# A packed feed-forward tail inside the logit group, a two-block K ring, and a re-tuned order: what it does to a kernel that TensorE bounds

## The chip, the cores and the metric

One core of one Trainium2 chip. The metric is the device time of one execution in microseconds (us), the median of several executions. Runs are with a granted TensorE clock of 0.99 or more.

## The reference, cut to what matters

One transformer layer without a second residual step: a layer norm feeds an attention branch and a gated feed-forward branch, and both are added to x. S is 2048, D is 512, 32 heads of 16, each position attends to 8 positions at distance 2, and the feed-forward width is **1376 = 10 x 128 + 96**. The inputs are bfloat16.

```python
x  = A_x
xn = layernorm(x)                       # no scale, no shift
# attention: q, k, v = xn @ wqkv; position s sees s, s-2, ..., s-14 (those >= 0)
logits = einsum("bhsd,bhswd->bhsw", q, k[idx]) * Dh**-0.5
o      = einsum("bhsw,bhswd->bhsd", softmax(masked logits), v[idx])
# feed-forward
h      = gelu(xn @ w_gate) * (xn @ w_up)        # 1376 columns
return x + o @ wo + h @ w_down
```

## The kernel before: the parts that matter

The kernel works on four blocks of 512 positions. A program in Python lists some 770 tasks with their engines, dependences and priorities, schedules them against a model of the chip, and emits each engine's instructions in the order found. So a change of a priority or of a model constant changes the order on every engine. A tile with a number (tile 4) is one of 16 of 128 positions each, four to a block; a column tile is a part of TensorE's array. A join is a place where TensorE needs what another engine has made.

TensorE does these groups: the QKV projection, the gate and up projections (11 pairs per block, the eleventh with 96 columns), the output and down projections (11 steps of 128, the last of 96), and two sorts of sums over products that VectorE has made and keeps in product buffers: the logits (`er`, 32 matmuls) and the value groups (`pvr`, 16 matmuls). The last two use weights of 32 columns, so that four matmuls run side by side on four column tiles. TensorE writes its results to a memory called PSUM, from where ScalarE and VectorE fetch them (an evacuation).

```python
        Wg = sb("Wg", [128, 4, DF], BF)          # DF = 1376
        Wu = sb("Wu", [128, 4, DF], BF)
        KT = sb("KT", [128, 4, PITCH], BF)       # K of all 2048 positions
        UNI = sb("UNI", [128, NUNI, 4, 512], BF) # NUNI = 10 product buffers
# ... the logit group of block b
                def mk_r(grp=list(er_grp), lg=it_lg):
                    def f(e):
                        for (g, prs) in grp:
                            for wq in range(2):
                                for sj in range(4):
                                    ins = e.matmul(PS[32 * sj:32 * sj + 32, ...],
                                        lhsT=E8[:, 24 - 8 * g:56 - 8 * g],
                                        rhs=UNI[:, prs[wq].slot, :, sj * 128:(sj + 1) * 128],
                                        start=(g == 0), stop=(g == 3), tile_position=(0, 32 * sj))
# ... gate and up of block b
            for j in range(NJ):                  # NJ = 11
                M = 128 if j < 10 else DF - 1280 # 96 columns in the last
                # 4 matmuls of 512 columns of x for gate, 4 for up; gelu and a copy on ScalarE,
                # one product on VectorE from SBUF
# ... the start: the order of tiles 0 to 3 on VectorE is fixed by hand
        chain(["bnst0", "bnag0", "ve0", "bnst1", "rstd0", "norm0", "bnag1", "ve1", "sub1", "bnst2", "rstd1",
               "norm1", "bnag2", "ve2", "sub2", "bnst3", "rstd2", "norm2", "bnag3", "ve3", "sub3", "rstd3",
               # ... cut
# ... the end of SyncE's stream
        if eng_name == "sp":
            for (s, tot) in self.dma_totals:     # 24 semaphores
                e.wait_ge(s, tot)
```

## Time and profile before

| | before |
|---|---|
| time, median of 3 runs (range) | 199.36 us (199.34 to 199.66) |
| span in the profile | 197.7 us |
| TensorE / VectorE / ScalarE / GpSimd busy | 97% / 75% / 53% / 6% |
| chain that ended last | 94% TensorE, 3% DMA, 1% VectorE |
| groups of 32-column tiles | 12, which makes 24 changes of tile form |

The first two rows differ by what lies outside the first and last instruction. The row to look at is the chain: from 8.4 us on it stays on TensorE, so the time is the start, plus what TensorE has to stream, plus the stretch after its last matmul. The lines of the profile are in the prediction. Timeline of the kernel before: start, length, engine, line, operation, what ended the idle time before it.

```profile
193.35 1.37 PE L1367 MATMUL PS<-Wd,HT 128*128 128x256 bf16 x11
194.83 0.42 DVE L1387 TENSOR_TENSOR OB<-PS,XR 128x256 bf16<-128x256 f32 x1 [1.19 <-PE PS L1367]
```

The span ends at 197.70, so 2.45 us follow the end of the last addition (195.25).

### The profile page before, as it was taken

The page shows a single profiled execution, that of the slowest core. Times are in us where ns is not written, and L with a number is a line of the kernel's source. Part 1 is how long each engine was busy: PE and PEld are TensorE (multiplying, and loading weights), DVE is VectorE, ACT ScalarE, POOL GpSimd, SP SyncE. Part 2 cuts the span into 40 slices and gives each one's busy share as a digit, 9 for nine tenths or more (in the row PEclk, how much of TensorE's full clock was granted, in tenths as well). Part 3 has the DMA queues.
Part 4 walks back from the last instruction along what each step waited for, and adds up shares of the span by engine and source line. Part 5 has one row for each costly group of instructions (what it writes and reads, how often), then busy time and mean ns, then how long its engine had stood idle before and what let it go on. Part 6 is the DMA issues. An engine that isn't in the chain of part 4 may idle for free.

```text
span 197.7 us, 3146 instructions
## 1 busy us (share of the span) xinstructions
PE 191.9 (97%) x1192; PEld 91.3 (46%) x1192; DVE 149.1 (75%) x230; ACT 105.0 (53%) x171; POOL 11.4 (6%) x32
## 2 busy tenths in 40 slices
PE   7799999999999999999999999999999999999993
PEld 2595444444444444444444444444444444444483
DVE  3789989999989999999879379995692986122131
ACT  4377459976737770075788104776792007776000
POOL 6420010130001000001000000000000000000000
DMA  4999998899327913529992535023953350010121
GB/s 120 363 385 385 276 154 182 224 210 165 108 53 177 224 33 102 159 82 171 222 176 46 119 122 133 0 58 103 234 100 93 89 153 27 0 55 3 53 66 40
DMA packets 33054, 27.02 MB, mean 137 GB/s; under 512 B 9392, under 2 KB 31504, under 8 KB 33040
## 3 DMA queue, kind: packets, MB, share of 16 engines
q1 hardware_dynamic: 33040, 26.83, 56.0%
q8 instruction: 9, 0.15, 0.3%
q14 instruction: 5, 0.04, 0.1%
HBM read 19.99 MB, written 5.26 MB: 128 GB/s over the span
## 4 chain that ended last, share of the span: by engine, by line
PE 94%; DMA 3%; DVE 1%; SPq 1%; issue 0%; DVEq 0%
PE PS L1316 39%; PE PS L1367 19%; PE PS L1087 18%; PE PS L1362 7%; PE PS L1285 4%; PE PS L1158 4%; PE PS L1043 3%; DMA XIN<-in_A_x_dram 3%; PE PS L995 0%; SPq L908 0%; DVE st L923 0%; SPq L860 0%; DVE OB L1387 0%; DVE XIN L970 0%; DVE rstd L946 0%
## 5 line engine op out<-in xcount | busy, mean ns | idle before, releaser
L1316 PE MATMUL PS<-xnT,Wu 128*128 128x512 bf16 (+1 forms) x176 | 44.6, 379 | 0.0
L1316 PE MATMUL PS<-xnT,Wg 128*128 128x512 bf16 (+1 forms) x176 | 44.4, 379 | 0.0
L1367 PE MATMUL PS<-Wd,HT 128*128 128x512 bf16 (+3 forms) x198 | 41.2, 356 | 0.0
L1264 DVE TENSOR_TENSOR UNI<-BS,PT 128x2048 bf16<-128x2048 bf16 x32 | 37.5, 1219 | 2.9 <-DMA PT<-pt_scratch 1.7
L1135 DVE TENSOR_TENSOR UNI<-QT,KT 128x2048 bf16<-128x2048 bf16 x32 | 37.2, 1219 | 0.5 <-PE PS L1285 0.2
L1087 PE MATMUL PS<-xnT,Wqkv 128*128 128x512 bf16 x160 | 36.2, 379 | 0.0
L1333 ACT ACTIVATE UU<-PS 128x512 bf16<-128x512 f32 (+1 forms) x44 | 26.4, 599 | 12.3 <-PE PS L1316 12.3
L1326 ACT ACTIVATE GG<-PS 128x512 bf16<-128x512 f32 (+1 forms) x44 | 26.3, 600 | 10.6 <-PE PS L1316 10.3
L1338 DVE TENSOR_TENSOR HT<-GG,UU 128x512 bf16<-128x512 bf16 (+1 forms) x44 | 17.4, 418 | 16.4 <-ACT UU L1333 16.4
L1367 PEld LDWEIGHTS PS<-Wd,HT 128*128 128x128 bf16 (+1 forms) x198 | 19.4, 98 | 18.7
L1316 PEld LDWEIGHTS PS<-xnT,Wg 128*128 128x128 bf16 (+1 forms) x176 | 17.2, 100 | 21.4 <-issue 1.3
L1316 PEld LDWEIGHTS PS<-xnT,Wu 128*128 128x128 bf16 (+1 forms) x176 | 17.4, 100 | 21.0 <-issue 0.8
L1087 PEld LDWEIGHTS PS<-xnT,Wqkv 128*128 128x128 bf16 x160 | 15.3, 98 | 19.4 <-ACT KT L1104 0.8
L1387 DVE TENSOR_TENSOR OB<-PS,XR 128x512 bf16<-128x512 f32 (+1 forms) x18 | 11.3, 630 | 15.9 <-PE PS L1367 15.9
L1111 ACT ACTIVATE VT<-PS 128x512 bf16<-128x512 f32 x16 | 9.5, 597 | 15.2 <-PE PS L1087 15.2
L1296 ACT ACTIVATE OT<-PS 128x512 bf16<-128x512 f32 x16 | 8.7, 594 | 16.3 <-PE PS L1285 16.3
L1362 PE MATMUL PS<-Wo,OT 128*128 128x512 bf16 (+1 forms) x72 | 16.8, 355 | 0.0
L1097 ACT ACTIVATE QT<-PS 128x512 bf16<-128x512 f32 x12 | 7.2, 597 | 12.7 <-PE PS L1087 12.7
L923 DVE BATCH_NORM_STATS2 st<-XIN 128x6 f32<-128x512 bf16 x16 | 10.4, 684 | 4.2 <-DMA XIN<-in_A_x_dram 4.2
L940 POOL TENSOR_TENSOR sq<-ve,mhalf 128x2 bf16<-128x2 f32 (+1 forms) x10 | 7.6, 763 | 77.7 <-DVE ve L934 77.7
L1362 PEld LDWEIGHTS PS<-Wo,OT 128*128 128x128 bf16 x72 | 7.0, 97 | 7.1
L1214 DVE TENSOR_REDUCE ms<-DE 128x128 f32<-128x1024 f32 x4 | 7.6, 1908 | 2.6 <-ACT DE L1209 2.6
(53 smaller groups left out, 114.9 us busy)
## 6 DMA issues: line engine op xcount, KB each, us to landing
BS<-vt_scratch SPq DMA_DIRECT2D x64, 128.5 KB, 3.3
vt_scratch<-VT SPq DMA_DIRECT2D x16, 128.0 KB
XR<-in_A_x_dram SPq DMA_DIRECT2D x16, 128.0 KB, 2.3
XIN<-in_A_x_dram SPq DMA_DIRECT2D x7, 256.0 KB, 3.9
out_dram<-OB SPq DMA_DIRECT2D x14, 128.0 KB, 2.0
Wqkv<-in_A_wqkv_dram SPq DMA_DIRECT2D x3, 512.0 KB
Wg<-in_B_w_gate_dram SPq DMA_DIRECT2D x1, 1376.0 KB, 6.5
Wu<-in_B_w_up_dram SPq DMA_DIRECT2D x1, 1376.0 KB, 11.1
```

What stands on the lines that cost most here:

```text
L923: return lambda e: e.bn_stats(out=st[:, t, :], in_=XIN[:, it.slot, t2, :])
L1087: ins = e.matmul(PS[:, 512 * it.slot:512 * it.slot + HWD], lhsT=lhsT, rhs=xnT[:, itx.slot, kt, c0:c0 + HWD], start=(kt == 0), stop=(kt == 3))
L1111: return lambda e: e.activation(out=VT[:, ito.slot, 0:HWD], in_=PS[:, 512 * it.slot:512 * it.slot + HWD], func=ACTF.Identity)
L1135: return lambda e: e.tensor_tensor(out=UNI[:, it.slot, :, :], in0=bass.AP(QT, (itq.slot * 4 + g) * 512, [[NQT * 4 * 512, 128], [0, 4], [1, ...
L1264: return lambda e: e.tensor_tensor(out=bass.AP(UNI, ito.slot * 2048, [[NUNI * 2048, 128], [512, 4], [128, 4], [1, 128]]), in0=bass.AP(BS, ...
L1316: ins = e.matmul(PS[0:M, 512 * it.slot:512 * it.slot + 512], lhsT=Wx[:, kt, j * 128:j * 128 + M], rhs=xnT[:, itx.slot, kt, :], start=(kt = ...
L1326: return lambda e: e.activation(out=GG[0:M, ito.slot, :], in_=PS[0:M, 512 * it.slot:512 * it.slot + 512], func=ACTF.Gelu_apprx_tanh)
L1333: return lambda e: e.activation(out=UU[0:M, ito.slot, :], in_=PS[0:M, 512 * it.slot:512 * it.slot + 512], func=ACTF.Identity)
L1338: return lambda e: e.tensor_tensor(out=HT[0:M, ito.slot, j, :], in0=GG[0:M, ig.slot, :], in1=UU[0:M, iu.slot, :], op=ALU.mult)
L1362: ins = e.matmul(PS[:, 512 * it.slot:512 * it.slot + CW], lhsT=OT[:, ito.slot, dq, ti * 128:(ti + 1) * 128], rhs=Wo[:, dq, c0:c1], start=( ...
L1367: ins = e.matmul(PS[:, 512 * it.slot:512 * it.slot + CW], lhsT=HT[0:K, ith.slot, j, ti * 128:(ti + 1) * 128], rhs=Wd[0:K, j, c0:c1], start ...
L1387: return lambda e: e.tensor_tensor(out=OB[:, ito.slot, 0:CW], in0=PS[:, 512 * it.slot:512 * it.slot + CW], in1=XR[:, itx.slot, c0:c1], op= ...
```

## The change

Its intent: (1) the 96 leftover columns of gate and up together need 8 of the long matmuls per block, each with a quarter of the array empty. The change packs them. Four matmuls with 128 columns of weights do 96 columns of gate and 32 of up; the other 64 of up are done by 8 matmuls of 64 weight columns by 256 columns of x, on two column tiles, at the head of the logit group, which uses small tiles anyway. (2) K is kept for two blocks instead of all four, with the 16 columns of overlap copied by GpSimd, and the room goes to two more product buffers. (3) The scheduler's model gets durations measured in a trace, one pass instead of several, and a table of priorities by group. Several weight pads are zeroed so that the down projection can use 128 rows throughout.

```diff
-        Wg = sb("Wg", [128, 4, DF], BF)
-        Wu = sb("Wu", [128, 4, DF], BF)
+        Wg = sb("Wg", [128, 4, 1280], BF)
+        Wu = sb("Wu", [128, 4, 1280], BF)
+        Wt = sb("Wt", [128, 4, 192], BF)
-        KT = sb("KT", [128, 4, PITCH], BF)
+        KT = sb("KT", [128, 2, 4, 528], BF)
-    NUNI = cfg.get("NUNI", 10)
+    NUNI = cfg.get("NUNI", 12)
@@ the logit group @@
+                        for kt in range(4):
+                            for c in range(2):
+                                ins = e.matmul(PS[64 * c:64 * c + 64, 512 * itu.slot:512 * itu.slot + 256],
+                                               lhsT=Wt[:, kt, 128:192],
+                                               rhs=xnT[:, itx.slot, kt, 256 * c:256 * c + 256],
+                                               start=(kt == 0), stop=(kt == 3), tile_position=(0, 64 * c))
                         for (g, prs) in grp:
@@ the tail: one group of 4 matmuls, one gelu, three products that read PSUM @@
+                        ins = e.matmul(PS[:, 512 * it.slot:512 * it.slot + 512], lhsT=Wt[:, kt, 0:128],
+                                       rhs=xnT[:, itx.slot, kt, :], start=(kt == 0), stop=(kt == 3))
+            for (nm, p0, n, g0, c0, c1, it_s) in (("a", 0, 32, 32, 0, 512, it_g), ("b", 0, 64, 64, 0, 256, it_u),
+                                                  ("c", 64, 64, 64, 256, 512, it_u)):
@@ the K ring @@
+                    return lambda e: e.tensor_copy(out=KT[:, i1.slot, :, 0:16], in_=KT[:, i0.slot, :, 512:528])
@@ the start @@
-        chain([..., "bnag1", "ve1", "sub1", "bnst2", "rstd1", "norm1", "bnag2", ...
+        chain([..., "bnag1", "ve1", "sub1", "rstd1", "norm1", "bnst2", "bnag2", ...
@@ scheduling @@
-        sched = dict(PE_SLACK=1.6, DMA_BPUS=250e3, TOL=dict(pe=0.3, act=-0.3, dve=0.0, pool=-0.3, sp=0.0))
-        G.schedule_passes(sched, cfg.get("NPASS", 3))
+        for t in G.tasks:
+            t.prio += shift_of(t.name)      # SHIFT: "acc0": 555, "h3": -1408, "qkv2": -3186, ... 23 entries
+        G.schedule(SCHED)
```

Cut: the loads of the tail's weights (three small ones), the zeroing of pads, durations of the model, dead code.

## The prediction

> **What bounds the kernel now.** I read the page's shares first, then the chain of waits, then TensorE's timeline, and last the first 16 us of all engines. Shares and slices:
>
> ```profile
> span 197.7 us, 3146 instructions
> PE 191.9 (97%) x1192; PEld 91.3 (46%) x1192; DVE 149.1 (75%) x230; ACT 105.0 (53%) x171; POOL 11.4 (6%) x32
> ...
> PE   7799999999999999999999999999999999999993
> ...
> DVE  3789989999989999999879379995692986122131
> ```
>
> A busy share of TensorE alone proves little, because matmul ends are modelled. The chain that ended last says the same, though:
>
> ```profile
> PE 94%; DMA 3%; DVE 1%; SPq 1%; issue 0%; DVEq 0%
> ```
>
> From 8.4 us to 194.7 us that chain never leaves TensorE, except for 0.12 us of issue at 98.95. So is it really streaming? Steps of the chain, start and length:
>
> ```profile
> 40.86 9.50 PE PS L1087 x44
> 50.35 6.04 PE PS L1316 x28
> 56.40 1.84 PE PS L1158 x32
> 58.24 1.83 PE PS L1316 x8
> ...
> 93.56 0.98 PE PS L1285 x16
> 94.53 4.42 PE PS L1316 x20
> ```
>
> 9.50/44 = 0.2159 and 6.04/28 = 0.2157 us for each matmul of 512 columns: a steady pitch of 0.216. The logit group (L1158) is 32 matmuls on 32-column tiles, four at a time: 8 x 0.216 = 1.73, and it takes 1.84. The group L1285 is 4 x 0.216 = 0.86 and takes 0.98. So each costs about 0.11 more, and so does the stretch after it (4.42 - 20 x 0.216 = 0.10): going into the four-tile form or out of it costs about 0.11 each time. There are 4 + 8 = 12 such groups, so 24 changes, 2.6 us in all. I add up every TensorE instruction from 8.73 us on, in program order: at 0.2158 per 512 columns, 0.0555 per 128, and 0.107 per change, the end comes out at 194.05. The trace has 194.73. Only 0.7 us is left for waits. The kernel is bound by how much TensorE has to stream, plus its start. Time beyond the end of TensorE (the last addition and store, and what lies outside the span) does not change.
>
> The start, all engines:
>
> ```profile
> 7.20 0.69 DVE L923 BATCH_NORM_STATS2 st<-XIN 128x6 f32<-128x512 bf16 x1 [1.20 <-DMA XIN<-in_A_x_dram]
> 7.99 0.35 DVE L970 TENSOR_SCALAR XIN<-XIN,rstd 128x512 bf16<-128x512 bf16 x1
> 8.40 0.40 PE L995 MATMUL PS<-ident,XIN 128*128 128x128 bf16 x4 [0.73 <-DVE XIN L970]
> 8.70 0.37 SPq L874 DMA_DIRECT2D Wg<-in_B_w_gate_dram  x1
> 8.73 1.96 PE L1043 MATMUL PS<-xnT,Wqkv 128*128 128x128 bf16 x32
> 11.12 0.35 DVE L970 TENSOR_SCALAR XIN<-XIN,rstd 128x512 bf16<-128x512 bf16 x1
> 11.39 1.28 DVE L923 BATCH_NORM_STATS2 st<-XIN 128x6 f32<-128x512 bf16 x2
> 11.64 0.39 PE L995 MATMUL PS<-ident,XIN 128*128 128x128 bf16 x4
> ```
>
> TensorE seems to wait for VectorE (L970, tile 1 of x) at 8.40. But the load of Wg may only be issued once the K weights have landed, and it is issued at 8.70; the first K projection starts at 8.73. So the K weights end this wait, whatever VectorE does. The trace's semaphore records agree: the sixteenth increment for the K weights comes at 8.68 us, that for the x load of tiles 4 and 5 (a part of block 1) at 10.91, that for tiles 6 and 7 at 11.62.
>
> **What the Trainium skill says.** "TensorE: Matmul & The Clock Gate", Wait — 56ns, not 53.3ns?: back-to-back matmuls of 512 columns start 215.7 ns apart at full clock. The trace has 0.216 and a granted clock of 1.00. "TensorEngine Tiling (Array Packing)", Tiling Modes / Key Properties: "Mode switching requires drain", and different tiles run in parallel; the same page lists 128x64 as two tiles and 128x32 as four. The trace agrees for four tiles (1.84 for 32 matmuls, and 0.11 per change). It has no 128x64 tile, so neither the overlap of two such tiles nor the cost of 64 to 32 is measured. "VectorE: DVE Perf Modes", The perf-mode tier table: tensor_tensor from PSUM runs at the lowest rate. The trace agrees: 689 ns for 128x512 from PSUM (L1387), 419 from SBUF (L1338).
>
> **The change part by part.** (1) Packed tail. Columns 1280 to 1375 of gate and up cost 4 + 4 matmuls per block now. After: 4 with 128 columns of weights (96 of gate and 32 of up), and 8 of 64 columns of weights by 256 of x, on two tiles, inside the logit group. If two tiles overlap as four do, the 8 take 4 x 0.108 = 0.43 where 4 x 0.216 = 0.86 stood. That is -0.43 per block, -1.73 in all. The down projection keeps 11 matmuls, padded with zeros. (2) Fewer groups. In the new order the logit groups of blocks 1 and 2 directly follow a group of L1285, so 10 groups stand alone where there were 12. If the step between 64- and 32-column tiles costs nothing: 20 changes for 24, -0.43. If it drains like the others: 3 + 3 for blocks 0 and 3, 4 + 4 for the two joined ones, 2 x 6 for the rest, 26, so +0.21. The skill's sentence speaks for the drain; I give it 0.7, which makes 0.7 x 0.21 - 0.3 x 0.43 = about 0. (3) Other engines. ScalarE loses 4 copies of 0.6 us. VectorE loses 4 products of 0.41 and gains per block one of 32x512 (0.69) and two of 64x256 (0.42 each) from PSUM: 4 x (1.53 - 0.41) = +4.5 us, 149 to 154 of 198. It is off the path as long as no join is late. (4) K ring, 12 product buffers: three small copies on GpSimd; the buffers let products run ahead. No time of their own.
>
> (5) The start. Tile 1's normalization moves before the statistics of tile 2, so its transposes can run at about 7.5 (the end of the first Q projection) instead of 8.40. That is worth nothing: the K weights still land at 8.68. But the new VectorE order also puts the statistics of tile 4 ahead of the last two steps of tile 3 (rstd, normalize), while the loads keep their order. VectorE is free for them at about 10.1 (tile 3's subtraction starts at 10.13 in the trace, and some 0.3 earlier once tile 1's two steps are out of its way) and then stands until tile 4's load at 10.91. From there: 0.69 for the statistics, to 11.65; aggregate, rstd and subtraction of tile 4 to about 12.2, by the starts of the same steps in the trace (0.2, 0.1, 0.3); normalize tile 3, 0.35, to 12.5. Its transposes come at 12.55 instead of 11.64. No other TensorE work stands ahead of them, so +0.9 us, and TensorE has no slack later to take it back.
>
> (6) The new schedule. With TensorE streaming without a gap I placed each group by adding up lengths, moved all by 0.9, and set VectorE's work in its new order beside it (1.15 us per 128x2048 product in a row, 1.22 for the 1024-wide steps). The tight joins: the L1285 group of block 1 and the logit group of block 2 right behind it need products that end about 1.1 us before; after the logit group of block 3, an up projection needs the two PSUM banks that the maximum and the subtraction free, about 0.3 us before; the others have 0.5 us and more. None is late on paper; I add 0.2 for what paper misses.
>
> Sum: -1.73 (packing) + 0 (changes of tile size) + 0.9 (start) + 0.2 (joins) = -0.6; 199.36 - 0.6 = 198.7.
>
> **The rivals.** One: the start doesn't lose, because tile 4's load lands before VectorE asks for it, or ScalarE hides it. Then -1.5 to -2.2, 197.2 to 197.9. For: the author's model was set by a trace. Against: the recorded landing at 10.91, and the program's order. Two: VectorE becomes the bound between 16 and 84 us, where it is busy 65.9 of 68.4 us and now gets the extra PSUM reads and whole-ring waits. For: 9s in nearly all slices there. Against: my walk has each join met, and the normalization of later blocks is what fills VectorE there, which can wait. It would make 199.5 to 202. Three: the two 64-column tiles do not overlap. Then 8 x 0.108 = 0.86, no gain from the packing, and 200.4. Against: the four-tile groups overlap fully. Four: the small weight loads (rows of 64 to 192 bytes) come late. They are needed at about 28 us, and Wu, which they follow, lands at 20.2 now; which leaves some 7 us for 192 KB and two waits in the queue.
>
> **Range and chances.** Below 196.5 it cannot well come: 199.36 - 1.73 - 0.43 - 0.7 (all waits of now gone). So faster by 2% (195.4) is nearly excluded. Slower by 2% (203.3) would take several missed joins at once. 198.7 us, 8 in 10 from 197.2 to 200.0; faster 0.02, same 0.94, slower 0.04.
>
> **What would show it.** The logit group with its 8 new matmuls at 2.3 us or a little more (packing right), or 2.7 (not overlapped); a gap of 0.9 us on TensorE before the last transposes, near 11.6 us, put down to VectorE's L967; the first K projection still at 8.7; a chain that stays on TensorE; the last matmul about 0.6 earlier than 194.7. The prediction is wrong if the chain goes over to VectorE in the middle, or if the start shows no gap.

## The result, and the profile after

| | before | after |
|---|---|---|
| time, median (range) | 199.4 us (199.34 to 199.66, 4 runs) | 198.33 us (197.96 to 198.55, 4 runs) |
| ratio to before, 95% interval | | 0.9942 (0.9924 to 0.996) |
| span in the profile | 197.7 us | 196.6 us |
| VectorE / ScalarE / GpSimd busy | 149.1 / 105.0 / 11.4 us | 153.6 / 103.6 / 21.4 us |

A ratio is the mean time of one kernel's fast runs over the mean of the other's fast runs of the same rounds, so it is not quite the ratio of the medians quoted. By the measure of 2% this is "same", as predicted, 0.4 us below the predicted 198.7. In the tables below, "K" is the start of the first K projection, "T" the start of the last transposes of the start (L995 before, L992 after), "A" the end of the last addition, "E" the end of the span, all read from the traces.

| us | K | K to T | T to A | A to E | E |
|---|---|---|---|---|---|
| before | 8.73 | 2.91 | 183.61 | 2.45 | 197.70 |
| after | 8.90 | 3.80 | 181.90 | 2.05 | 196.65 |
| difference | +0.17 | +0.88 | -1.71 | -0.40 | -1.06 |

The start grew, the middle and the end shrank. First, the page of the changed kernel, its span, busy times and chain (share of the span by engine):

```profile
span 196.6 us, 3169 instructions
PE 188.7 (96%) x1189; PEld 90.6 (46%) x1208; DVE 153.6 (78%) x238; ACT 103.6 (53%) x167; POOL 21.4 (11%) x37
...
PE 91%; DMA 4%; SPq 1%; DVE 1%; issue 1%; ACT 0%; DVEq 0%
```

Still a chain of TensorE. It leaves TensorE once in the middle, at 130.2 us, for 1.0 us of ScalarE and VectorE; there the records around the seam of two groups stand 0.54 us apart instead of the 0.31 to 0.32 of other such seams, just one pitch of 0.216 more, and the group has 3 recorded matmuls where the program has 4. So a record is missing, and TensorE did not wait. (The profile of e4_both below lacks no record; there the same seam stands at 0.31.) **The start**, timeline of the changed kernel:

```profile
8.90 1.96 PE L1040 MATMUL PS<-xnT,Wqkv 128*128 128x128 bf16 x32 [0.90 <-DMA Wqkv<-in_A_wqkv_dram]
...
11.08 0.70 DVE L920 BATCH_NORM_STATS2 st<-XIN 128x6 f32<-128x512 bf16 x1 [0.38 <-DMA XIN<-in_A_x_dram]
...
12.29 0.35 DVE L967 TENSOR_SCALAR XIN<-XIN,rstd 128x512 bf16<-128x512 bf16 x1
...
12.70 0.40 PE L992 MATMUL PS<-ident,XIN 128*128 128x128 bf16 x4 [0.72 <-DVE XIN L967]
```

VectorE stands 0.38 us until the load of tile 4 lands, does its statistics, and only then normalizes tile 3 (12.29), for which TensorE waits. Before, those transposes ran at 11.64 without a wait. **The middle**, the chain of the changed kernel (start, length, piece):

```profile
28.75 0.86 PE PS L1361 x4
29.62 0.56 PE PS L1161 x8
30.17 1.84 PE PS L1168 x32
...
98.85 0.98 PE PS L1295 x16
99.82 0.56 PE PS L1161 x8
100.38 1.84 PE PS L1168 x32
```

L1161 is the packed tail: 0.56 us. Eight matmuls of 256 columns two at a time are 4 x 0.108 = 0.43, and 0.13 remain for going over to 64-column tiles. The logit group behind it still takes 1.84 and not 1.73, so going from 64- to 32-column tiles costs 0.11 too. In the second half of the fence a group of L1295 runs straight into the tail and the logits; the joined groups save one change of form, and the new step gives it back. **The end**, timeline of the changed kernel:

```profile
192.70 1.36 PE L1405 MATMUL PS<-Wd,HT 128*128 128x256 bf16 x11
194.18 0.42 DVE L1425 TENSOR_TENSOR OB<-PS,XR 128x256 bf16<-128x256 f32 x1 [1.18 <-PE PS L1405]
```

TensorE's last group starts 0.65 earlier, the span ends 1.06 earlier. The missing 0.40 lies after the last addition, where I had said that nothing would change.

### The profile page after: what moved, and what is told of

Read it like the earlier page. It is cut to its first block, busy times and chain, and to the rows that moved or that the text cites. A ratio compares the mean times of both kernels' runs of the same rounds, so it can differ in the third digit from the quotient of the medians.

```text
span 196.6 us, 3169 instructions
## 1 busy us (share of the span) xinstructions
PE 188.7 (96%) x1189; PEld 90.6 (46%) x1208; DVE 153.6 (78%) x238; ACT 103.6 (53%) x167; POOL 21.4 (11%) x37
## 4 chain that ended last, share of the span: by engine, by line
PE 91%; DMA 4%; SPq 1%; DVE 1%; issue 1%; ACT 0%; DVEq 0%
PE PS L1326 35%; PE PS L1405 19%; PE PS L1084 18%; PE PS L1401 7%; PE PS L1168 4%; DMA XIN<-in_A_x_dram 4%; PE PS L1295 3%; PE PS L1040 2%; PE PS L1361 2%; PE PS L1161 1%; SPq L859 1%; SPq L905 0%; DVE st L920 0%; ACT UU L1343 0%; SPq L909 0%
## 5 line engine op out<-in xcount | busy, mean ns | idle before, releaser
L1405 PE MATMUL PS<-Wd,HT 128*128 128x512 bf16 (+1 forms) x197 | 41.3, 355 | 0.1
L1326 PE MATMUL PS<-xnT,Wu 128*128 128x512 bf16 x158 | 40.2, 379 | 0.1
L1326 PE MATMUL PS<-xnT,Wg 128*128 128x512 bf16 x153 | 39.6, 379 | 0.7 <-issue 0.3
L1336 ACT ACTIVATE GG<-PS 128x512 bf16<-128x512 f32 x40 | 24.0, 600 | 23.7 <-PE PS L1326 23.7
L1343 ACT ACTIVATE UU<-PS 128x512 bf16<-128x512 f32 x40 | 23.9, 601 | 7.7 <-PE PS L1326 7.7
L1405 PEld LDWEIGHTS PS<-Wd,HT 128*128 128x128 bf16 x198 | 19.4, 98 | 18.7
L1348 DVE TENSOR_TENSOR HT<-GG,UU 128x512 bf16<-128x512 bf16 x40 | 15.8, 415 | 12.4 <-ACT UU L1343 11.8
L1326 PEld LDWEIGHTS PS<-xnT,Wg 128*128 128x128 bf16 x160 | 15.3, 98 | 19.8 <-ACT UU L1343 0.8
L1326 PEld LDWEIGHTS PS<-xnT,Wu 128*128 128x128 bf16 x160 | 15.5, 98 | 19.2 <-ACT GG L1336 0.4
L1124 POOL COPY KT<-KT 128x64 bf16<-128x64 bf16 x3 | 9.4, 3118 | 7.7 <-ACT KT L1101 6.0
```

What stands on the lines that cost most here:

```text
L1326: ins = e.matmul(PS[0:M, 512 * it.slot:512 * it.slot + 512], lhsT=Wx[:, kt, j * 128:j * 128 + M], rhs=xnT[:, itx.slot, kt, :], start=(kt = ...
L1336: return lambda e: e.activation(out=GG[0:M, ito.slot, :], in_=PS[0:M, 512 * it.slot:512 * it.slot + 512], func=ACTF.Gelu_apprx_tanh)
L1343: return lambda e: e.activation(out=UU[0:M, ito.slot, :], in_=PS[0:M, 512 * it.slot:512 * it.slot + 512], func=ACTF.Identity)
L1348: return lambda e: e.tensor_tensor(out=HT[0:M, ito.slot, j, :], in0=GG[0:M, ig.slot, :], in1=UU[0:M, iu.slot, :], op=ALU.mult)
L1405: ins = e.matmul(PS[:, 512 * it.slot:512 * it.slot + CW], lhsT=HT[:, ith.slot, j, ti * 128:(ti + 1) * 128], rhs=Wd[:, j, c0:c1], start=Fal ...
```

## The experiments

Twelve runs. Two more builds never ran: tripled products into one destination and 8 matmuls of the tail into two accumulations of one bank were refused by the check for races and memory (no record of them is kept), and were replaced by e9_dve1, e9_dve2 and e13_onetile.

| run | time, us (runs) | ratio to before | K | K to T | T to A | A to E |
|---|---|---|---|---|---|---|
| a0_after | 197.90 (5) | 0.9924 (0.9909 to 0.9939) | 8.51 | 3.85 | 181.90 | 2.05 |
| e1_start | 197.13 (4) | 0.9887 (0.9868 to 0.9906) | 8.56 | 2.91 | 181.89 | 2.05 |
| e2_oneside | 198.00 (5) | 0.9929 (0.9916 to 0.9942) | 8.77 | 3.79 | 181.94 | 2.05 |
| e3_tile32 | 197.31 (4) | 0.9893 (0.988 to 0.9907) | 8.32 | 3.84 | 181.33 | 2.05 |
| e13_onetile | 199.68 (6) | 1.0014 (0.9992 to 1.0036) | 8.45 | 3.84 | 183.60 | 2.04 |
| e4_both | 196.57 (4) | 0.9852 (0.9829 to 0.9875) | 8.73 | 2.91 | 181.25 | 2.05 |
| e10_swap | 196.72 (4) | 0.9861 (0.9839 to 0.9884) | 8.96 | 2.91 | 181.19 | 2.04 |
| e12_before4 | 198.87 (6) | 0.9973 (0.9955 to 0.9992) | 8.25 | 2.91 | 184.03 | 2.11 |
| e9_dve1 | 198.22 (6) | 0.9928 (0.9902 to 0.9953) | 8.70 | 3.81 | 181.91 | 2.05 |
| e9_dve2 | 199.03 (6) | 0.9976 (0.995 to 1.0003) | 8.27 | 3.84 | 182.99 | 2.05 |
| e6_noshift | 202.20 (4) | 1.0146 (1.0099 to 1.0193) | 8.29 | 3.84 | 185.60 | 2.04 |
| e7_uni10 | 201.89 (6) | 1.0131 (1.0096 to 1.0167) | 8.50 | 3.85 | 185.38 | 2.07 |

The kernel before had medians of 199.43, 199.45 and 199.41. K wanders between 8.25 and 8.96 from profile to profile, with the landing of the K weights or the first steps before it; that is a scatter, and the columns to its right are freed of it. (In e10_swap, K is the start of the second and third projections, of which the Q projection comes first.)

### a0_after: the changed kernel again

No edit.

> The changed kernel once more, for pairing on the same chip. Expected 198.3 us (197.9 to 198.6), ratio to the kernel before 0.994. In its profile: a gap of 0.7 to 0.9 us on TensorE before the last transposes near 12 us, the 64-column group at 0.56 us, a chain that never goes over to VectorE in the middle. If the further 0.4 us by which the first measurement beat the sum of the prediction came from a quick end of the program, the stretch from the last addition to the end of the span will scatter between the two kernels; if the schedule brought them, the last matmul ends 0.4 us earlier than before for a reason to be found in the middle.

197.90 us. K to T, T to A and A to E agree with the first profile within 0.05 us; only K is 0.39 earlier. So the 0.40 at the end is no scatter (2.05 in every profile of the changed program so far), and neither is the -1.71 of the middle. The answer to the alternative in the expectation is "both": the end gives 0.40, the middle is as the prediction's terms say, which is worked out below.

### e1_start: undo one step of the new order at the start

```diff
         G.schedule(SCHED)
+        dv = G.order["dve"]
+        # bnst4, bnag4, sub4 (tile 4) go behind norm3 in VectorE's order
+        for k, t in enumerate(late):
+            dv.remove(t)
+            dv.insert(dv.index(by["norm3"]) + 1 + k, t)
```

> Only VectorE's order at the start is altered: statistics, aggregate and subtraction of tile 4 come after the normalization of tile 3. My theory: VectorE stood waiting for tile 4's load with tile 3's last two steps behind it, and TensorE, which never has slack later, lost 0.9 us by it. Expected 197.4 us (0.9 less than the changed kernel of the same call), the last transposes near 11.8 instead of 12.7 us, and no gap before them. Rival A: the gap only moves, because the late load of tile 4 then holds up the transposes of block 1 or VectorE's dense stretch to 84 us: 198.3, no gain. Rival B: the landing of the K weights at 8.7 to 8.9 us sets the start anyway: no gain, the last transposes still at 12.7.

197.13 us, 0.77 below the changed kernel by the medians; by the traces K to T falls from 3.85 to 2.91 and T to A stays. Timeline of this run:

```profile
11.48 0.39 PE L992 MATMUL PS<-ident,XIN 128*128 128x128 bf16 x4
```

No gap before it. The theory holds, and the loss is not merely moved: nothing later takes the 0.94 back or gives it up. Rivals A and B fall.

### e2_oneside and e13_onetile: is it the overlap of two tiles that pays?

```diff
-                        for kt in range(4):
-                            for c in range(2):
+                        for c in range(2):
+                            for kt in range(4):
```

> The 8 matmuls of 64 weight columns by 256 columns of x are the same, but no longer alternate between the two column tiles: four on one tile, then four on the other. Theory: the packing pays only because neighbours in the order sit on different tiles and run side by side. Then each of the 4 groups takes 8 x 0.108 = 0.86 instead of 0.43 us, and the time rises by 1.7 us, to 200.0. Rival A: TensorE starts a later matmul of the free tile ahead of its turn, or two tiles of 64 columns don't overlap at all and the gain came from elsewhere: no difference, 198.3. Rival B: part of it, one pair at the seam of the two halves overlaps: 7 steps of 0.108 instead of 4, +1.3.

198.00 us against 197.90, and T to A differs by 0.04: no difference. My theory falls in the form I gave it: neighbours in the program need not be on different tiles. The chain of this run:

```profile
29.48 0.57 PE PS L1161 x8
```

The single records say more. With alternating tiles the starts come in pairs 3 to 4 ns apart, and a pair every 0.11 us. Here they also come in pairs, 13 to 14 ns apart. That is four steps of 3.4 ns, as if the four of one tile were handed over first, and then the first of the other tile starts while three of its forerunners still wait. (The records don't name the tile.) That still left open whether overlap is behind it at all, so the next run takes the second tile away:

```diff
-                            for c in range(2):
-                                ins = e.matmul(PS[64 * c:64 * c + 64, 512 * itu.slot:512 * itu.slot + 256], ...
-                                               rhs=xnT[:, itx.slot, kt, 256 * c:256 * c + 256],
-                                               ..., tile_position=(0, 64 * c))
+                            ins = e.matmul(PS[0:64, 512 * itu.slot:512 * itu.slot + 512], lhsT=Wt[:, kt, 128:192],
+                                           rhs=xnT[:, itx.slot, kt, 0:512],
+                                           start=(kt == 0), stop=(kt == 3), tile_position=(0, 0))
```

> The run with the one-sided order showed no loss (0.57 us for the group instead of the expected 0.86; its records start in pairs 13 ns apart, one of each tile, although the program has all four of one tile first). So either the two tiles work through their own queues side by side whatever the order (theory), or the group is simply cheap and no overlap is behind it (rival). Here all of the tail goes to one tile: 4 matmuls of 64 weight columns by 512 columns of x into the same 64 partitions, the same multiplications, the same outputs, with the products reading from there. Theory: 4 x 0.216 = 0.86 us for the group instead of 0.43, +0.43 in each block, +1.7 us in all, 199.7 if the changed kernel is at 198.0 on this chip. Rival: no difference, 198.0.

199.68 us; T to A is 183.60, which is 1.70 more. The chain of this run:

```profile
29.21 0.98 PE PS L1160 x4
```

0.98 = 4 x 0.216 + 0.11, against 0.56. So the same multiplications on one tile cost 0.42 more in each block, and the packing's gain is the overlap of two tiles, whatever the order of the two in the program.

### e3_tile32: the tail in the tile form of its neighbour

```diff
                         for kt in range(4):
-                            for c in range(2):
-                                ins = e.matmul(PS[64 * c:64 * c + 64, ...], lhsT=Wt[:, kt, 128:192],
-                                               ..., tile_position=(0, 64 * c))
+                            for q in range(4):
+                                c, w = q // 2, q % 2
+                                ins = e.matmul(PS[32 * q:32 * q + 32, ...], lhsT=Wt[:, kt, 128 + 32 * w:160 + 32 * w],
+                                               ..., tile_position=(0, 32 * q))
```

> The packed tail is cut into four tiles of 32 columns (16 matmuls of 32 weight columns by 256 of x) instead of two of 64, so that it has the tile form of the logit group behind it. Four at a time, the 16 take 4 x 0.108 = 0.43 us, as the 8 did. Theory: a change from 64-column to 32-column tiles drains like any other (0.11 us); it goes away 6 times (4 times between tail and logits, twice between the L1295 group and the tail): -0.66 us, 197.7. Rival: the change between two column-tile forms is free, and the 0.13 us beyond 0.43 that the trace shows belongs to the 64-column matmuls themselves: no difference, 198.3. A third way: 16 matmuls of 32 columns cost more to issue than 8 of 64 (+0.1 each, 4 times): 198.1.

197.31 us, 0.59 below the changed kernel; T to A falls by 0.57. TensorE itself gains more: from T to its last matmul the trace is 0.71 shorter, but the last addition then waits for a store from its buffer and starts 0.52 us behind the start of the last matmul, in the changed kernel 0.38. The chain, first at a tail that stands alone and then at one behind a group of L1296 (lines moved by one):

```profile
29.09 0.55 PE PS L1162 x16
29.64 1.73 PE PS L1169 x32
...
98.94 0.44 PE PS L1162 x16
99.38 1.73 PE PS L1169 x32
```

The logit group is down to 8 x 0.216 = 1.73, and behind another group of 32-column tiles the tail is down to 4 x 0.108 = 0.43. So a change between two column forms costs the 0.11 us of a change to the full array, and 16 small matmuls stream as fast as 8. This holds in the same kernel with the same outputs: a gain that the change left on the table.

### e4_both and e10_swap: the two gains together, and one try more

e4_both is e1_start and e3_tile32 in one. e10_swap is e4_both with two neighbours exchanged in TensorE's order:

```diff
         G.schedule(SCHED)
+        # Q projection of tile 1 ahead of the K projection of tile 0
+        pe[i], pe[i + 1] = b, a
```

> The start edit and the 32-column tail together. One path and two different places on it, so the two gains add up: -0.77 and -0.59 as measured give 196.5 us (ratio to the kernel before 0.9855). If the two share something (for instance if the earlier start makes VectorE late for a group that the shorter tail brings forward), less: 196.8 to 197.1.

> On top of both, TensorE does the Q projection of tile 1 before the K projection of tile 0. Now it waits for the K weights (0.9 us idle until 8.5 to 8.9). Tile 1's transposed x is there at 8.64 in the first profile of the changed kernel. If the wait for the K weights is the last to end in the start, about 0.1 to 0.2 us come off: 196.3 to 196.4. If the evacuation of tile 1 ends no earlier than the K weights land (in the repeat they landed at 8.5), nothing: 196.5, or even a loss of 0.1.

e4_both: 196.57 us, ratio 0.9852. The gains add up (K to T of e1_start, T to A of e3_tile32), and its list of waits holds nothing of TensorE's after the start. (The last addition waits for a store here too: 0.45 us behind the start of the last matmul.) It is the fastest version here, 0.9852 of before and 1.3 us below the changed kernel's 197.90. It was run at another time. e10_swap: 196.72, no gain (the intervals overlap). Timeline of e4_both, then of e10_swap:

```profile
8.73 1.96 PE L1040 MATMUL PS<-xnT,Wqkv 128*128 128x128 bf16 x32 [0.89 <-DMA Wqkv<-in_A_wqkv_dram]
```

```profile
8.96 1.96 PE L1040 MATMUL PS<-xnT,Wqkv 128*128 128x128 bf16 x32 [0.69 <-ACT xnT L1003]
```

The wait for the K weights is gone and a wait for ScalarE's evacuation of tile 1 stands in its place, in a run whose start was some 0.4 us later anyway (the transposes of tile 1 at 7.89 instead of 7.46). Two waits end nearly together there; taking away one is worth nothing that these runs can see.

### e12_before4: the 0.40 us at the end

```diff
             for (s, v) in t.waits:
                 e.wait_ge(s, v)
+            if t.name in EXTRA_WAIT:        # two loads and two stores around 141 to 168 us, kernel before
+                e.wait_ge(self.order["pool"][0].sem, 1 + EXTRA_WAIT.index(t.name))
```

> A test of the end of the program, on the kernel before. Between the end of the last addition and the end of the span lie 2.45 us in the kernel before and 2.05 in all five profiles of the changed one. SyncE's records differ by one hold-up of 0.36 to 0.38 us, at its 207th recorded instruction in both programs: in the kernel before that is the branch after all waits, in the changed one, which has four more SyncE instructions, a wait while the last store is still under way. Here the kernel before gets four waits more in SyncE's stream, all met long ago, at loads and stores around 141 to 168 us. Theory (a hold-up at a fixed place in the stream, which falls behind the last store's flight): 2.05 to 2.1 us after the last addition, time 199.05 instead of 199.4. Rival (something else in the changed kernel's end, for instance which semaphores the last stores use): no difference, 2.45.

198.87 us against 199.45, and A to E falls from 2.45 to 2.11. The pauses between SyncE's recorded instructions, counted from 0 (ns before the instruction; from the traces):

```
no.       203  204  205  206  207  208  209  210   what no. 207 is
before     62   53  550   42  376  138  145    -   the branch behind all waits
after      63   53   42   42  371   55   31   40   a wait, while the last store is under way
before+4   62   53   42   42  362   55  172   39   a wait, while the last store is under way
10 bufs    31   62   48   42  357   58  140  145   the last of the waits (e7_uni10)
```

No. 207 is held for 0.36 to 0.38 us in each of these programs, and in all 14 traces kept, wherever it falls. (The 550 in the first row and the 172 in the third are the wait for the last store.) In the kernel before it comes after the store has landed and adds to the span; with four instructions more in the stream it comes while the store is still flying and costs nothing. So this part of the gain has nothing to do with the change's intent: its three loads and one more wait pushed the stream along. The profile does not say what holds the instruction. In all 14 traces one packet of 8 KB of the queue that the page calls "q14 instruction" starts 0.61 to 0.91 us after no. 207 does. So the place seems tied to the loading of instructions; but that packet comes after the hold, and the cause stays open. The time fell by 0.58 where 0.34 is explained; the interval of the ratio reaches to 0.9992, and 0.34 of 199.45 would be 0.9983, so this is within it. T to A of this profile is 0.42 longer and K 0.48 earlier than in the profile of before, and the one eats up the other at a single join. The value group near 99 us starts at the same time in both, since VectorE makes its product only after a load (VectorE starts at 96.57 before, at 96.51 here). Timeline of the kernel before, then of e12_before4:

```profile
99.07 1.05 PE L1285 MATMUL PS<-UNI,E 128*32 128x512 bf16 x16
```

```profile
99.02 1.05 PE L1290 MATMUL PS<-UNI,E 128*32 128x512 bf16 x16 [0.54 <-DVE UNI L1269]
```

By the starts of the records, TensorE comes to this group 0.50 us after the matmul before it in the kernel before and 0.92 here, against 0.31 at the other such seams. So it waits 0.19 and 0.61.

### e9_dve1 and e9_dve2: how far is VectorE from the path?

```diff
+        # in VectorE's task pv1_1_1, ahead of the product; once in e9_dve1, twice in e9_dve2
+        e.tensor_reduce(out=dmy[:, k:k + 1], in_=Wg[:, 0, 0:1024], axis=AX.X, op=ALU.max)
```

> How far is VectorE from the path? Ahead of the last product of value groups that the joined groups of block 1 and 2 wait for, VectorE does one more reduction (128 x 1024 from SBUF to one column, estimated at 1.1 to 1.3 us from the 1.22 us of its 1024-wide steps). In the profile of the changed kernel TensorE asks for that product's result 1.45 us, and for the next one's 1.3 us, after VectorE has made it. Theory: all of it is absorbed: 198.0 us, as the changed kernel on this chip. Rival (VectorE is the hidden bound there): the extra time comes out at the end, +1.1, 199.1.

> The same with two such reductions, 2.2 to 2.5 us. Theory: 1.3 us are absorbed, the rest stops TensorE at the joined groups near 98.8 us and is not taken back: +0.8 to +1.2, 198.8 to 199.2. Rival A (VectorE is the bound): +2.2 to +2.5. Rival B (TensorE's groups there have slack of their own, or later groups take it back): 198.0.

e9_dve1: 198.22 us and T to A 181.91, the same as without: 1.2 us of more work on VectorE vanish. e9_dve2: 199.03 us and T to A 182.99, so 1.08 of 2.34 us come out. Timeline of e9_dve2:

```profile
95.49 2.34 DVE L1446 TENSOR_REDUCE dmy<-Wg 128x1 f32<-128x1024 bf16 x2
...
99.11 1.05 PE L1296 MATMUL PS<-UNI,E 128*32 128x512 bf16 x16 [0.86 <-DVE UNI L1275]
```

2.34 - 1.08 = 1.26 were absorbed, which is the slack of 1.3 us that the trace showed between the product and its use. What is beyond the slack is not taken back in the 95 us that follow. So VectorE, busy 78%, is off the path but not far from it at this join.

### e6_noshift and e7_uni10: what the order is worth

```diff
-SHIFT = {"acc0": 555, ...}
+SHIFT = {}
```

> The changed kernel without the table of priorities by group; its scheduler then makes another order on every engine. 12 groups of small tiles stand alone (10 in the changed kernel), so 28 changes of tile form instead of 26: +0.2. Theory: TensorE's work is the same otherwise, so only joins that come late can cost more; with nothing tuned some do: 198.5 to 201, with gaps on TensorE put down to VectorE. Rival: the order hardly matters as long as TensorE has something to stream: 198.2.

```diff
-    NUNI = cfg.get("NUNI", 12)
+    NUNI = cfg.get("NUNI", 10)
```

> The changed kernel with 10 product buffers instead of 12, all else equal; the scheduler then moves some groups, and the joining of two logit groups to a group of L1295 is lost (28 changes of tile form instead of 26: +0.2). Theory: the two buffers' own worth is that little plus at most one late join: 198.2 to 198.8. Rival: the ring and the buffers are what carries the gain, as products can no longer run ahead: 199.4 or more, TensorE waiting for VectorE's products.

e6_noshift: 202.20 us, e7_uni10: 201.89 us; both over the top of what I expected, and for e7_uni10 the rival had it. TensorE's list of waits (line and what it waited for: us in total, times, longest), first e6_noshift, then e7_uni10:

```profile
PE PS L1397 <- DVE HT L1344: 2.6, 2, 1.5
```

```profile
PE PS L1295 <- DVE UNI L1274: 1.9, 1, 1.9
...
PE PS L1161 <- DVE UNI L1138: 0.8, 1, 0.8
```

In e6_noshift the down projection waits twice for VectorE's last gate-up products. In e7_uni10 a value group waits 1.9 us at 142 us and the packed logit group 0.8 us at 100 us, both for products. T to A is 3.7 and 3.5 longer than in the changed kernel; the named waits and 0.2 for two more changes of form make up 2.8 and 2.9 of that, and the rest is spread over small waits. So joins met on time are a property of this one order, made with this table and these 12 buffers together. What the runs don't show is that 10 buffers would be too few with a table of their own: the kernel before has 10, and its longest wait on TensorE after the start is the 0.19 us at 99.07 (told under e12_before4).

## Why the prediction was right, and where it was off

The predicted sum was -0.6 us, the measured one -1.06 (spans), and all its terms can be set beside a measurement.

- **Packed tail, -1.73: right.** The group took 0.56 of which 0.43 is streaming, as worked out; the same work on one tile cost +1.70 (e13_onetile). The rival "two tiles don't overlap" is out.
- **Changes of tile size, about 0 as an average of two cases: the likelier case came true**, +0.21 for 26 changes at the flat 0.107. Read from the starts of the records, they cost more: 24 x 0.110 before and 26 x 0.115 after, so +0.36. The step from 64- to 32-column tiles costs like the others (e3_tile32: six such steps gone, -0.71 up to TensorE's last matmul, -0.57 up to A and -0.59 in time, against 6 x 0.107 = 0.64). The average hid a choice that could have been made by design: four tiles instead of two.
- **The start, +0.9: right**, by its own steps. K to T went from 2.91 to 3.80; VectorE waited for tile 4's load until 11.08 (predicted 10.91), and the last transposes came at 12.70 (predicted 12.55), the rest being K, 0.17 later in this run. VectorE stood for 0.38 us and not for the predicted 0.8, because it came there later: tile 2's normalization took 0.75 us instead of 0.35, at the same time as GpSimd's new zeroing of HT. That cost nothing, as the load ended the wait. Undoing the step gave 0.77 us in time and 0.94 in K to T (e1_start). The first rival is out. That the earlier normalization of tile 1 is worth nothing was right too.
- **Joins, +0.2 for what paper misses: wrong in sign.** With the changes counted, TensorE's streaming from T to the end of the last matmul adds up to 182.44 us before and 180.92 after; the traces have 182.91 and 181.21. So 0.47 us beyond that sum became 0.29: -0.19 instead of +0.2. Only a part of it is waiting. By the starts of the records, TensorE of the kernel before has one late join after T, the value group at 99.07 (0.19 us, and 0.04 just behind it; the prediction read it as 0.12 us of issue), and that of the changed kernel has none: -0.23. Another 0.11 us of before stands at and just behind the 16 places where a down projection ends with 96 rows of weights; padded to 128 rows, they take no longer than others. The rest is that changes of form cost more than 0.107. The slack on paper was real, 1.26 us at the tightest large join (e9_dve2), and the second rival, VectorE as the bound, is out for this order. Late joins of its kind come back when the table or the two buffers are taken away (T to A 3.7 and 3.5 us longer, e6_noshift and e7_uni10).
- **"Time beyond the end of TensorE does not change": wrong**, -0.40. This is the step that failed. I took the stretch after the last addition as a constant of the program; a hold-up at a fixed place in SyncE's stream of instructions lay in it, and the change moved it out (e12_before4).
- **The rest.** VectorE went from 149.1 to 153.6 us, +4.5 as predicted; a new product of 64x256 from PSUM took 0.42 us as assumed:

```profile
32.38 0.42 DVE L1376 TENSOR_TENSOR HT<-GG,PS 64x256 bf16<-64x256 bf16 x1
```

The small weight loads came in time (no wait at L1361), so the fourth rival is out.

The sum in measured terms: -1.73 (packing) + 0.36 (changes of form) - 0.23 (join) - 0.11 (rows) + 0.88 (start) - 0.40 (end) + 0.17 (K in this run) = -1.06. What had been estimated as -0.6 came out lower by the end (-0.40), the joins (-0.43, from +0.2 to -0.23) and the rows (-0.11), and higher by the changes of form (+0.36) and K (+0.17). These errors, 0.94 one way and 0.53 the other, partly cancel; that the predicted 198.7 came so near is in part luck. Of the change's real gain of 1.7 us in the middle, half was given back in the start by one statistics step put ahead of a load, and more than a third of the net gain (0.40 of 1.06) is an accident of the end.

## What to carry to other kernels

When one engine streams without a gap, the time is a sum: count its instructions by length, count its changes of tile form, and look at the two ends by themselves, where an order or a single instruction that nobody meant can be worth a good part of a clever packing (0.88 and 0.40 us here, against 1.73). Small matmuls packed beside others should take the tile form of their neighbours, since every change of form cost about 0.11 us here. An order made by a scheduler belongs to its inputs: a buffer count or a priority taken away alone shows what that order needs, not what the buffer is worth.

## What the Trainium skill lacked or had wrong

- "TensorEngine Tiling (Array Packing)", Tiling Modes / Key Properties, says that a change of tiling mode drains TensorE, without a cost, and lists 128x64 and 128x32 as two configurations without saying whether a step between them counts. Here each change cost about 0.11 us at full clock, and so did that step: the logit group took 1.84 us behind 64-column tiles and 1.73 behind 32-column tiles.
- "TensorE: Matmul & The Clock Gate", Part 3, The mechanism, calls matmuls strictly first in, first out, without reordering. In e2_oneside four matmuls of one tile stand in the program ahead of four of the other, and the group took 0.57 us, as with alternating tiles, with starts in pairs 13 to 14 ns apart; strict order would need at least 7 x 0.108 = 0.76 us. On one tile the work took 0.98.
- "SBUF — State Buffer", Who interferes with whom: a VectorE instruction with two SBUF inputs contends with a GpSimd one that reads SBUF, and the loser is blocked for the whole instruction. Here the 128x64 copy of the K ring, recorded as 0.24 us when VectorE did no products (at 64 us), took at about 18 us 1.29 us in nine of twelve profiles, until 0.10 us after the end of one product, which fits the page. But beside the row of eight products at 49 us the same copy took 0.32 to 0.49 us in eight profiles, 0.87 in one and 7.82 in three, far more than one product (1.2 us). The page does not say that a whole row can pass ahead of it. Nothing waited for the copy. Timeline of a0_after and of e2_oneside, the same copy:

```profile
49.74 7.82 POOL L1124 COPY KT<-KT 128x64 bf16<-128x64 bf16 x1 [5.97 <-ACT KT L1101]
```

```profile
49.96 0.34 POOL L1124 COPY KT<-KT 128x64 bf16<-128x64 bf16 x1 [5.96 <-ACT KT L1101]
```

- "Runtime: NRT & Kernel Launch", Instruction fetch mechanics, says that instructions are refilled in blocks and that crossing a block's boundary is mostly hidden. Neither it nor another page has a hold-up of 0.36 to 0.38 us at a fixed count of SyncE's instructions (record 207, counted from 0, in all 14 traces), nor that it lies bare at the end of a program when it falls behind the last store. Whether the two belong together is not shown.
